# Attention and a two-layer projection: the products with V in one run per pair of heads, and a list scheduler with new durations and priorities

## The chip, the cores and the metric

One core of a Trainium2 chip runs the kernel. The metric is device time in microseconds, the median of the runs of one program; lower is better.

## The reference

Two parts follow each other. The first is attention for 8 batches and 8 heads, 576 tokens, head size 64, float32. A score counts where the query's block of 64 tokens is not ahead of the key's. The second takes the attention's result as 4608 tokens of 512 features. `w_in`, `w_out` and `g_ln` reach the chip as float64 words.

```python
scores = scale * np.matmul(q, k.transpose(0, 1, 3, 2))       # scale = 1/sqrt(64)
scores = np.where(block_i >= block_j, scores, -1000000000.0)
attn = np.exp(scores - np.max(scores, axis=-1, keepdims=True))
attn = attn / (np.sum(attn, axis=-1, keepdims=True) + 1e-09)
x = np.matmul(attn, v)                                       # then (tokens, 512)
h = x @ w_in                                                 # (4608, 1024)
e = np.exp(h - np.max(h, axis=-1, keepdims=True))
solu = h * (e / (np.sum(e, axis=-1, keepdims=True) + 1e-09))
mu, var = mean and variance of solu over its 1024 features
out = ((solu - mu) / np.sqrt(var + 1e-06) * g_ln) @ w_out    # (4608, 512)
```

## The kernel before

**Attention** (`attention(p)`, from L376) works on a pair of heads; there are 32 pairs, four to a batch. q and k are loaded and transposed on TensorE (L400). For the first four pairs the scores are float32 products (L441); for the others q and k are split into two float32r parts each, and the scores are sums of two products (L449, L445). VectorE takes each row's maximum (L469), ScalarE the exponential with its sum (L473), VectorE the reciprocal (L480, L481), and GpSimd scales the probabilities (L488; L489 is the same on VectorE, open for the first four pairs). 25 transposes in seven groups turn the probabilities around (L499); each group is copied from PSUM into `pt` by ScalarE (L371).

The **products with V** (L533) are float32, with 64 columns of weights: the two heads lie side by side in the array, which is used as two halves (128*64 in the profile; everything else is 128*128). The result of a pair has two parts, `ph` 0 (four products of two instructions) and `ph` 1 (ten products of two). Each part is an operation of its own, with its own PSUM slot and its own list of copies it waits for: `ph` 0 needs only the first two groups of transposes. The results go into `xt` (L371), which holds three batches.

**The projections** (`moe(t, key)`, from L549) take 36 tiles of 128 tokens. x is split into two float32r parts (`xh` L564 and `xl` L568), `h` is 24 matmuls in two halves (L589), then come maximum (L595), exponential (L596), product with its sum (L597), subtraction of the mean (L599), squares (L601), the reciprocal root (L612), eight transposes of `u` (L624, called `ct`), the split into `ch` and `cl` (L628, L629), 24 matmuls of `o` (L637), the scaling on the way out of PSUM (L641) and the store (L643).

**The weights** are prepared once, in 16 pieces (`prep`, L315 to L336): float64 words to float32 in five steps on ScalarE, VectorE and GpSimd (L322, L323, a scaling by 2^-112 at L324 to L326, L327, L328, L329), a product with g for `w_out` (L331, L332), a cast to the upper part (L333, L334) and a subtraction for the lower part (L335, L336). They use the tiles `ub`, `ob` and `xt[2]`, which the projections and the third batch need later.

**The order of all instructions** is set at build time by `Schedule`. Every operation has an engine, a duration, the tiles it reads and writes, and a key. `run` steps through modelled time; an engine that is free takes, among the operations whose inputs are ready and for which a PSUM slot is free, the one with the lowest key. `alts` names other engines that can do an operation, with a penalty added to the key; an alternative is only open if its penalty is under 3. PSUM has two slots of two banks ("D") and four of one bank ("S"). Each engine then runs its own list in that order, and waits by semaphores; SP issues nearly all loads. The key of an operation of attention is the pair's number p plus an offset of `PARAMS` (`K["pt"] + p` for the transposes of the probabilities, names with `32` for the first four pairs); that of an operation of tile t is `4 + K["h0"] + t * K["hs"]` plus an offset (`K["h"]`, `K["o"]`, `K["ct"]`); that of weight piece n is `K["w0"] + K["w1"] * n`. What the products with V add to the list in each pair:

```python
for ph in range(2):
    av = newps("S")
    js = range(5) if ph else range(2)
    ...
    sel = [c for c in ptc if (c[1] <= 6) == (ph == 0)]
    ptk = [(x, p % NPT, c0) for x in ("pt", "pt2") for c0, _ in sel]
    op("PE", 54 + sum(t_two(64 * mov(j, 0, ph)[2], True) for j in js), avmm, r=ptk + [f"vr{i}"], key=kk, opens=av)
```

Of the kernel before, what the change touches and what calls it, by code (L numbers as in the profile page):

```python
# [31 lines left out]
NPT = 2  # L32
START = {"PE": 0.0, "ACT": 2930.0, "DVE": 0.0, "POOL": 2500.0, "SP": 560.0}
PARAMS = {
# [6 lines left out]
    "a_sp32": -5.767, "a_lf": -3.555, "a_w": 15.208, "a_xh": 37.196, "a_xl": 48.757, "a_c": 6.341,  # L41
    "a_o": 13.796, "ns32": 4, "np": 32, "l0": -6.655, "a_cl": 5.076,
# [7 lines left out]
class Schedule:  # L50
    """Orders the operations of all engines: a list schedule over their dependences, with
    durations from shapes alone. PSUM slots (of one or two banks) are given out as it goes,
    and an operation that several engines can do goes to the one that is free for it first."""
# [10 lines left out]
    def op(self, eng, dur, fn, r=(), w=(), key=0.0, opens=None, ps=None, tail=0.0, alts=()):  # L64
# [3 lines left out]
        for e, d, f, pen in alts:  # L68
            if pen < 3:
                o.alts[e] = (d, f, key + pen)  # L70
        o.succ, o.npred, o.pre, o.opens, o.done = [], 0, [], opens, False
        o.idx = len(self.ops)
        o.uses = ps if ps is not None else opens
        preds = set()
        r, w = list(r), list(w)
        if o.uses is not None:
            self.users[o.uses] = self.users.get(o.uses, 0) + 1
            (w if eng == "PE" else r).append(("ps", o.uses))
# [18 lines left out]
    def run(self):  # L97
# [5 lines left out]
        engfree = {e: START[e] for e in engs}  # L103
        events = [(t, i, 0, None, None) for i, t in enumerate(sorted(START.values()))]
# [12 lines left out]
        while events:  # L117
            t = events[0][0]
            while events and events[0][0] <= t:
                _, _, kind, o, e = heapq.heappop(events)  # L120
                if kind == 1:
                    for s in o.succ:
                        s.npred -= 1
                        s.pre.append((t, o.eng))
                        if s.npred == 0:
                            ready(s, t)
                    if o.uses is not None:
                        left[o.uses] -= 1
                        if left[o.uses] == 0:
                            heapq.heappush(events, (t + LAT[o.eng]["PE"], n, 3, o, None))  # L130
                            n += 1
                elif kind == 2:
                    pend[e].append((o.alts[e][2], o.idx, o))
                elif kind == 3:
                    free[self.kind[o.uses]].append(self.slot[o.uses])
            for e in engs:
# [4 lines left out]
                for _, _, o in pend[e]:  # L141
                    if o.opens is not None:
                        if not free[self.kind[o.opens]]:
                            continue
                    elif o.uses is not None:
                        until = max([v for x, v in held[o.uses].items() if x != e], default=0.0)
# [11 lines left out]
                if best.opens is not None:  # L158
                    self.slot[best.opens] = free[self.kind[best.opens]].pop(0)
                    held[best.opens] = {}  # L160
                if best.uses is not None:
                    held[best.uses][e] = t + best.dur + 128
# [12 lines left out]
def kernel(  # L175
# [45 lines left out]
    # upper parts (its last 128 columns: 64 of the last queries, 64 zeros), then lower parts  # L221
# [4 lines left out]
    # tiles of queries: (head, i) is 128 rows of one head, LAST the last 64 of both heads  # L226
# [20 lines left out]
    # the scores of the first pairs are float32 products  # L247
# [14 lines left out]
    # the table of functions is loaded, and the clock of the tensor engine raised, while the  # L262
    # first loads are under way
# [16 lines left out]
    def newps(kind):  # L280
        vid[0] += 1
        sc.kind[vid[0]] = kind
        return vid[0]
# [4 lines left out]
    def t_mm(n):  # L288
        return max(107.0, n / 2.4 + 2.5)
# [4 lines left out]
    def t_two(n, fp32=False):  # L294
        # two products with 64 rows of output each, side by side in the array
        return max(224.0, n / 0.6 + 29) if fp32 else max(106.0, n / 2.4 + 53.0)
# [19 lines left out]
    def prep(i, src, hi, lo, gcol, name, key):  # L316
# [6 lines left out]
        op("DVE", 335, lambda: DVE.tensor_scalar(out=T2, in0=high, scalar1=TOP, scalar2=-TOP, op0=ALU.min, op1=ALU.max), r=[kr_], w=[k2], key=key)  # L323
        op("ACT", 520, lambda: ACT.activation(T2, T2, AF.Copy, scale=DOWN), r=[k2], w=[k2], key=key,  # L324
           alts=[("POOL", 588, lambda: POOL.tensor_scalar(out=T2, in0=T2, scalar1=DOWN, scalar2=1.0, op0=ALU.mult, op1=ALU.mult), K["a_cl"]),
                 ("DVE", 335, lambda: DVE.tensor_scalar(out=T2, in0=T2, scalar1=DOWN, scalar2=None, op0=ALU.mult), K["a_lf"])])  # L326
        op("DVE", 335, lambda: DVE.tensor_scalar(out=T1.bitcast(U32), in0=T2.bitcast(U32), scalar1=3, scalar2=0x7FFFFFF8, op0=ALU.logical_shift_left, op1=ALU.bitwise_and), r=[k2], w=[k1], key=key)  # L327
        op("DVE", 602, lambda: DVE.scalar_tensor_tensor(out=T1.bitcast(U32), in0=T2.bitcast(U32), scalar=0x80000000, in1=T1.bitcast(U32), op0=ALU.bitwise_and, op1=ALU.bitwise_or), r=[k1, k2], w=[k1], key=key)  # L328
        op("POOL", 1225, lambda: POOL.tensor_tensor(out=T1.bitcast(I32), in0=T1.bitcast(I32), in1=T3.bitcast(I32), op=ALU.add), r=[k1, k3], w=[k1], key=key)  # L329
        if gcol is not None:  # L330
            op("ACT", 613, lambda: ACT.activation(T1, T1, AF.Copy, scale=gcol), r=[k1, "gt"], w=[k1], key=key,  # L331
               alts=[("DVE", 400, lambda: DVE.tensor_scalar(out=T1, in0=T1, scalar1=gcol, scalar2=None, op0=ALU.mult), K["a_lf"])])  # L332
        op("ACT", 520, lambda: ACT.activation(hi, T1, AF.Copy), r=[k1], w=[(name, "h")], key=key,  # L333
           alts=[("DVE", 335, lambda: DVE.tensor_copy(hi, T1), K["a_lf"])])  # L334
        op("POOL", 1225, lambda: POOL.tensor_tensor(out=lo, in0=T1, in1=hi.bitcast(F32), op=ALU.subtract), r=[k1, (name, "h")], w=[(name, "l")], key=key,  # L335
           alts=[("DVE", 602, lambda: DVE.tensor_tensor(out=lo, in0=T1, in1=hi.bitcast(F32), op=ALU.subtract), K["a_w"])])  # L336
# [16 lines left out]
    # score tiles in PSUM: kind, [(unit, column)], [(first masked column, step, count)]  # L353
# [8 lines left out]
    # columns of the sums, by the two batches of reciprocals  # L362
# [6 lines left out]
    def copy(which, n_, aps, scale, w, key, ps, r=()):  # L369
        # a copy out of PSUM, on either engine  # L370
# [3 lines left out]
    def attention(p):  # L374
# [27 lines left out]
        # the last tile of kr is [k's last 64 tokens; q's last 64 tokens]  # L402
# [285 lines left out]
```

## Time and profile before

| | |
|---|---|
| median of 3 runs | 816.08 us (815.44 to 816.29) |
| span of the profiled execution | 814.3 us (its own time is not given beside it) |
| TensorE busy | 787.6 us, 97% |
| ScalarE busy | 557.0 us, 68% |
| VectorE busy | 492.3 us, 60% |
| GpSimd busy | 308.6 us, 38% |
| largest shares of the chain that ended last | `o` L637 24%, `h` L589 23%, products with V L533 10%, transposes of probabilities L499 9%, scores L449 8% |

The span runs from the first to the last instruction of one execution. A busy share is a mean over stages: the start, where weights are prepared and the first pairs run, the long middle, where a pair and a tile alternate, and the end, where only tiles are left. TensorE's matmuls are pipelined, so their durations overlap; what a matmul costs is read from the distance of starts, or from the chain of waits.

### The profile page before, as it was taken

What the parts mean: (1) busy time and instruction counts of PE and PEld (TensorE: products, weight loads), DVE (VectorE), ACT (ScalarE), POOL (GpSimd) and SP (SyncE); (2) the same over time, 40 slices, a digit from 0 to 9 for tenths busy, and PEclk for the clock granted to TensorE, in tenths of its full rate; (3) what the DMA queues carried; (4) which work ended last, traced back from release to release, by engine and by line L of the source; (5) the groups of instructions that cost most, each with busy time, mean ns of one, the idle gap of its engine ahead of it and who ended that gap; (6) DMA issues with size and microseconds to landing.
All of it is one profiled execution on the core that took longest, in us unless ns stands there. A gap on an engine that the chain in (4) does not pass through costs nothing.

```text
span 814.3 us, 14121 instructions
## 1 busy us (share of the span) xinstructions
PE 787.6 (97%) x4711; PEld 635.9 (78%) x4711; DVE 492.3 (60%) x1200; ACT 557.0 (68%) x1441; POOL 308.6 (38%) x468
## 2 busy tenths in 40 slices
PE   6878899999999999999999999999999999999998
PEld 5545678888888888888888888888888888788886
DVE  5999986655665555566665555555666655333332
ACT  6778787686877777777787777777777777434332
POOL 3567772243443323333333323233333333132210
PEclk9999999999999999999999999999999999999999
DMA  7457534143443343333333333433343320000000
GB/s 210 117 146 181 140 83 105 49 102 82 109 101 92 88 101 101 93 95 96 94 90 79 83 94 87 101 101 96 92 101 88 95 63 29 14 27 26 14 27 39
DMA packets 132760, 71.84 MB, mean 88 GB/s; under 512 B 118864, under 2 KB 118864, under 8 KB 132688
## 3 DMA queue, kind: packets, MB, share of 16 engines
q1 hardware_dynamic: 131632, 70.68, 34.0%
q8 instruction: 37, 0.61, 0.3%
q10 hardware_dynamic: 1056, 0.26, 0.2%
q14 instruction: 35, 0.29, 0.1%
HBM read 36.70 MB, written 9.44 MB: 57 GB/s over the span
## 4 chain that ended last, share of the span: by engine, by line
PE 86%; DVE 9%; issue 2%; ACT 1%; POOL 1%; DMA 0%; SPq 0%; DVEq 0%; POOLq 0%
PE ps L637 24%; PE ps L589 23%; PE ps L533 10%; PE ps L499 9%; PE ps L449 8%; PE ps L624 5%; PE ps L400 3%; PE ps L445 3%; DVE nm L469 2%; DVE pb L489 1%; DVE xt L326 1%; DVE xt L328 1%; DVE xt L327 1%; PE ps L441 1%; DVE ks L420 1%
## 5 line engine op out<-in xcount | busy, mean ns | idle before, releaser
L488 POOL TENSOR_SCALAR pb<-pb,rz 128x512 f32<-128x512 f32 (+4 forms) x270 | 148.8, 571 | 179.0 <-DVE rz L481 164.1
L473 ACT ACTIVATE pb<-ps,nm 128x128 f32<-128x128 f32 (+4 forms) x288 | 155.7, 551 | 61.6 <-DVE nm L469 61.5
L469 DVE TENSOR_REDUCE nm<-ps 128x1 f32<-128x128 f32 (+4 forms) x288 | 133.0, 504 | 4.3 <-PE ps L445 1.2
L599 POOL TENSOR_SCALAR ub<-ub,ms 128x1024 f32<-128x1024 f32 x36 | 41.0, 1140 | 190.0 <-DVE ms L598 190.0
L499 PE MATMUL ps<-ident,pb 128*128 128x128 f32 x800 | 106.0, 275 | 7.1 <-ACT pb L473 3.3
L371 ACT ACTIVATE pt<-ps 128x512 f32<-128x512 f32 (+1 forms) x224 | 108.7, 553 | 4.9 <-PE ps L499 4.3
L499 PEld LDWEIGHTS ps<-ident,pb 128*128 128x128 f32 x800 | 92.6, 141 | 23.3 <-ACT pb L473 3.6
L533 PE MATMUL ps<-pt,vr 128*64 128x320 f32 (+4 forms) x896 | 101.3, 366 | 0.7 <-ACT pt L371 0.5
L533 PEld LDWEIGHTS ps<-pt,vr 128*64 128x64 f32 x896 | 58.8, 137 | 41.7 <-issue 5.5
L449 PE MATMUL ps<-ks,qs 128*128 128x384 f32 (+1 forms) x448 | 84.5, 328 | 1.7 <-DMA qs<-qs 1.2
L589 PE MATMUL ps<-wih,xh 128*128 128x512 f32 x288 | 82.2, 407 | 2.9 <-DVE qtl L428 2.9
L637 PE MATMUL ps<-woh,ch 128*128 128x512 f32 x288 | 83.6, 411 | 0.0
L629 DVE TENSOR_TENSOR cl<-ps,ch 128x512 fp32r<-128x512 f32 x72 | 49.3, 685 | 56.6 <-ACT ch L628 56.6
L589 PE MATMUL ps<-wil,xh 128*128 128x512 f32 x288 | 79.6, 399 | 0.0
L637 PE MATMUL ps<-wol,ch 128*128 128x512 f32 x288 | 79.0, 396 | 0.0
L637 PE MATMUL ps<-woh,cl 128*128 128x512 f32 x288 | 78.8, 395 | 0.0
L589 PE MATMUL ps<-wih,xl 128*128 128x512 f32 x288 | 78.2, 393 | 0.0
L449 PEld LDWEIGHTS ps<-ks,qs 128*128 128x128 f32 x448 | 68.6, 191 | 7.2 <-ACT xh L564 1.0
L641 ACT ACTIVATE ob<-ps,ms 128x512 f32<-128x512 f32 x36 | 24.7, 687 | 71.5 <-PE ps L637 66.6
L596 ACT ACTIVATE ub<-ps,ms 128x1024 f32<-128x1024 f32 x36 | 40.1, 1115 | 46.2 <-DVE ms L595 46.1
L589 PEld LDWEIGHTS ps<-wil,xh 128*128 128x128 f32 x288 | 54.9, 191 | 12.9
L637 PEld LDWEIGHTS ps<-woh,cl 128*128 128x128 f32 x288 | 54.1, 188 | 13.0
(79 smaller groups left out, 1238.6 us busy)
## 6 DMA issues: line engine op xcount, KB each, us to landing
qs<-qs SPq DMA_DIRECT2D x56, 288.0 KB, 4.1
out_dram<-ob SPq DMA_DIRECT2D x36, 256.0 KB, 2.0
qr<-in_q_dram SPq DMA_DIRECT2D x64, 128.0 KB, 3.0
vr<-in_v_dram SPq DMA_DIRECT2D x64, 128.0 KB, 2.5
ks<-k2h SPq DMA_DIRECT2D x56, 144.0 KB, 2.5
kr<-in_k_dram SPq DMA_DIRECT2D x62, 128.0 KB, 2.7
ub<-in_moe_w_in_dram SPq DMA_DIRECT2D x8, 512.0 KB, 3.6
ub<-in_moe_w_out_dram SPq DMA_DIRECT2D x8, 512.0 KB, 3.7
```

The lines of the kernel that those rows point to most:

```text
L371: op("ACT", t_act(n_), lambda: ACT.activation(aps()[0], aps()[1], AF.Copy, scale=scale), r=r, w=w, key=key, ps=ps, alts=[("DVE", t_dve(n_) ...
L449: PE.matmul(t[:, off : off + wid[u]], qs[h][:, 640 * n_ + 128 * i_ : 640 * n_ + 128 * i_ + 128], ks[h][:, 0 : wid[u]], start=n_ == 0, stop ...
L469: op("DVE", t_dve(wid[u]), lambda sp=sp, off=off, u=u: DVE.tensor_reduce(out=nm_[u], in_=PS(sp)[:, off : off + wid[u]], axis=AX.X, op=ALU. ...
L473: op("ACT", t_act(wid[u], 186), lambda sp=sp, off=off, u=u, zg=zg, zc=zc: ACT.activation(pb[:, poff[u] : poff[u] + wid[u]], PS(sp)[:, off ...
L488: op("POOL", 0.836 * nn + 243, lambda b=b, nn=nn, zg=zg, zc=zc: POOL.tensor_scalar(out=pb[:, poff[b] : poff[b] + nn], in0=pb[:, poff[b] : ...
L499: PE.transpose(t[:, (s_ - c0) * P : (s_ - c0 + 1) * P], pb[:, poff[b] + j * P : poff[b] + (j + 1) * P], ident)
L533: PE.matmul(PS(av)[half[h], 64 * o_ : 64 * (o_ + n_)], vt[:, j, 64 * h : 64 * h + 64], pt_.rearrange("p s q -> p (s q)")[:, 128 * s_ + 64 ...
L589: PE.matmul(o_, a_[:, c, :], w_[:, c, s_], start=(si == 0 and c == 0), stop=(si == 2 and c == NKI - 1))
L599: op("POOL", 1097, lambda: POOL.tensor_scalar(out=u, in0=u, scalar1=m[:, 3:4], scalar2=1.0, op0=ALU.add, op1=ALU.mult), r=[uk, ("m3", i)], ...
L624: PE.transpose(t_[:, c * P : (c + 1) * P], u[:, (4 * hf + c) * P : (4 * hf + c + 1) * P], ident)
L629: op("DVE", t_dve(512), lambda cs=cs, cps=cps: DVE.tensor_tensor(out=cl[:, cs, :].rearrange("p c q -> p (c q)"), in0=PS(cps), in1=ch[:, cs ...
L637: PE.matmul(o_, a_[:, c, :], w_[:, c, :], start=(hf == 0 and si == 0 and c == 0), stop=(hf == 1 and si == 2 and c == 7))
```

## The change

1. The products with V of both parts become one operation: it opens two one-bank PSUM slots, waits for all seven copies of transposed probabilities, and issues its 28 instructions in a row.
2. `Schedule` can open several PSUM slots for one operation. It keeps the tiling that TensorE was last used in and adds `SWITCH` = 130 ns to an operation in the other one (`mode`). It treats GpSimd and the operations of VectorE marked `port` as users of one resource: while one runs, the other's aren't started.
3. Durations of the model: 24 matmuls of a projection at 231.5 ns instead of 216, scores and products with V by new formulas.
4. All offsets of `PARAMS` are new. Penalties that cross the bound of 3: `a_lf` (casts, the scaling by 2^-112 and the product with g on VectorE) -3.6 to 122.9, closed; `a_cl` (that scaling on GpSimd) 5.1 to -88.3, open; `a_w` (the weights' subtraction on VectorE) 15.2 to -51.8, open; `a_o` (the outputs' scaling on VectorE) 13.8 to -121.7, open.

Nothing that is computed changes, nor any shape of an instruction. The core of the diff:

```diff
+SWITCH = 130.0
 PARAMS = {
-    "nd": 2, "ld": 50.439, "lv": 1.808, "q": -3.52, "qe": 1.142, "s": 6.097, "se": -34.711, "sr": -9.155,
-    "sp": -24.637, "pt": -53.902, "pe": -29.441, "av": -40.478, "ae": -54.031, "x": -19.096, "h0": 30.197,
-    "hs": 1.049, "h": 10.087, "he": 5.197, "c": 29.273, "sq": 24.027, "ct": -50.339, "ce": -26.902,
-    "o": 12.508, "oe": 52.668, "w0": 4.753, "w1": 3.56, "q32": -49.338, "qe32": 2.512, "s32": -30.884,
-    "se32": -21.58, "sr32": -9.773, "sp32": 10.661, "pt32": -1.589, "pe32": 9.069, "av32": -26.682,
-    "ae32": -42.402, "ld32": 8.508, "lv32": 16.251, "e0": 19.063, "e1": 23.219, "e2": 43.479, "a_sp": 40.963,
-    "a_sp32": -5.767, "a_lf": -3.555, "a_w": 15.208, "a_xh": 37.196, "a_xl": 48.757, "a_c": 6.341,
-    "a_o": 13.796, "ns32": 4, "np": 32, "l0": -6.655, "a_cl": 5.076,
+    "nd": 2, "ld": 67.63, "lv": -39.691, "q": 8.023, "qe": 9.533, "s": -24.887, "se": -34.498,
+    "sr": -111.106, "sp": -24.343, "pt": -134.132, "pe": -125.475, "av": -34.899, "ae": -72.798,
+    "x": -37.528, "h0": -8.482, "hs": 0.492, "h": 132.7, "he": -68.376, "c": 83.463, "sq": 117.471,
+    "ct": -171.804, "ce": 39.0, "o": 33.813, "oe": 81.677, "w0": -14.772, "w1": 7.585, "q32": 2.115,
+    "qe32": -27.97, "s32": -13.067, "se32": -42.156, "sr32": 115.054, "sp32": 29.952, "pt32": 73.492,
+    "pe32": -3.409, "av32": -11.716, "ae32": -160.724, "ld32": 53.733, "lv32": 90.552, "e0": 39.854,
+    "e1": 108.665, "e2": 81.5, "a_sp": 145.727, "a_sp32": -6.778, "a_lf": 122.869, "a_w": -51.778,
+    "a_xh": 13.907, "a_xl": 186.098, "a_c": 45.054, "a_o": -121.701, "ns32": 4, "np": 32, "l0": -100.944,
+    "a_cl": -88.339,
 }
...
+                    port = e == "POOL" or e == "DVE" and o.port
+                    if port and portfree > t:
+                        heapq.heappush(events, (portfree, n, 0, None, None))
+                        n += 1
+                        continue
+                    if o.opens:
+                        kinds = [self.kind[x] for x in o.opens]
+                        if any(len(free[k]) < kinds.count(k) for k in kinds):
                             continue
...
+                if e == "PE" and best.mode != mode:
+                    best.dur += SWITCH
+                    mode = best.mode
+                if e == "POOL" or e == "DVE" and best.port:
+                    portfree = t + best.dur
...
-        for ph in range(2):
-            av = newps("S")
-            js = range(5) if ph else range(2)
-
-            def avmm(av=av, js=js, ph=ph):
+        avs = [newps("S"), newps("S")]
+
+        def avmm():
+            for ph, js in ((0, range(2)), (1, range(5))):
                 for j in js:
...
-            sel = [c for c in ptc if (c[1] <= 6) == (ph == 0)]
-            ptk = [(x, p % NPT, c0) for x in ("pt", "pt2") for c0, _ in sel]
-            op("PE", 54 + sum(t_two(64 * mov(j, 0, ph)[2], True) for j in js), avmm, r=ptk + [f"vr{i}"], key=kk, opens=av)
+        ptk = [(x, p % NPT, c0) for x in ("pt", "pt2") for c0, _ in ptc]
+        op("PE", sum(t_two(64 * mov(j, 0, ph)[2], True) for ph, js in ((0, range(2)), (1, range(5))) for j in js), avmm, r=ptk + [f"vr{i}"], key=kk, opens=tuple(avs), mode=1)
+        for ph in range(2):
+            av = avs[ph]
...
-            op("PE", 12 * 216, hmm, r=wk + [("xh", i), ("xl", i)], key=key + K["h"], opens=hps if hf == 0 else None, ps=hps)
+            op("PE", 12 * 231.5, hmm, r=wk + [("xh", i), ("xl", i)], key=key + K["h"], opens=hps if hf == 0 else None, ps=hps)
```

## Rows read from the trace of the kernel before

**Rows 1.** The page's first part: busy time, share of the span and instructions of each engine.

```profile
PE 787.6 (97%) x4711; PEld 635.9 (78%) x4711; DVE 492.3 (60%) x1200; ACT 557.0 (68%) x1441; POOL 308.6 (38%) x468
```

**Rows 2.** Busy time of each engine by stretches (start to end), granted clock, DMA share, GB/s.

```profile
0.00:20.00 20.00, 12.71 (x59) 9.83 (x60) 11.47 (x32) 12.29 (x33) 7.42 (x23) 1.00 0.79 210
20.00:40.00 20.00, 16.79 (x77) 11.51 (x77) 19.44 (x42) 14.55 (x39) 10.54 (x10) 0.92 0.47 123
40.00:60.00 20.00, 14.82 (x87) 9.39 (x88) 19.35 (x48) 15.89 (x51) 13.23 (x12) 1.00 0.48 129
60.00:80.00 20.00, 16.75 (x128) 11.79 (x128) 19.56 (x36) 17.08 (x43) 14.21 (x15) 0.95 0.72 184
80.00:100.00 20.00, 16.89 (x85) 12.50 (x82) 19.53 (x37) 13.62 (x38) 16.19 (x17) 0.88 0.54 138
100.00:120.00 20.00, 19.50 (x125) 15.60 (x124) 18.01 (x44) 18.01 (x47) 15.15 (x18) 1.00 0.34 84
...
426.00:448.40 22.40, 22.40 (x143) 18.42 (x142) 13.48 (x35) 16.35 (x44) 7.95 (x13) 1.00 0.38 94
```

**Rows 3.** Chain of waits, 400 to 475 us: start us, us, what (a pair's products, L533).

```profile
430.27 0.80 PE ps L533 x8
431.07 0.59 PE ps L624 x4
431.66 2.21 PE ps L533 x20
```

**Rows 4.** Chain of waits, 780 to 815 us: same columns.

```profile
786.34 5.59 PE ps L589 x24
...
801.20 0.44 PE ps L624 x4
```

**Rows 5.** TensorE: line L533 alone (ns min/median/max, first and last), then timeline 0 to 150 us.

```profile
L533 PE MATMUL ps<-pt,vr x896: 218/381/797, 30.4 to 701.1; 128*64 128x320 f32 x76, 128*64 128x256 f32 x26, 128*64 128x128 f32 x26, 128*64 128x192 f32 x26
...
61.70 2.93 PE L533 MATMUL ps<-pt,vr 128*64 128x320 f32 x28 [0.49 <-ACT pt L371]
64.56 2.62 PE L499 MATMUL ps<-ident,pb 128*128 128x128 f32 x19
```

**Rows 6.** The page's groups: copies of transposed probabilities out of PSUM (busy, mean ns).

```profile
L371 ACT ACTIVATE pt<-ps 128x512 f32<-128x512 f32 (+1 forms) x224 | 108.7, 553 | 4.9 <-PE ps L499 4.3
```

**Rows 7.** Instructions by line, 0 to 115 us: count, busy us, mean ns, idle before.

```profile
L326 DVE TENSOR_SCALAR xt<-xt 128x512 f32<-128x512 f32 x16 | 14.4, 918 | 0.1
...
L328 DVE SCALAR_TENSOR_TENSOR xt<-xt 128x512 uint32<-128x512 uint32 x16 | 12.1, 758 | 0.1
...
L322 ACT ACTIVATE ob<-ub 128x512 int32<-128x512 uint32 x16 | 10.7, 679 | 0.0
...
L334 DVE CAST woh<-xt 128x512 fp32r<-128x512 f32 x5 | 4.6, 917 | 0.1
...
L332 DVE TENSOR_SCALAR xt<-xt,gt 128x512 f32<-128x512 f32 x4 | 4.2, 1054 | 0.0
...
L334 DVE CAST wih<-xt 128x512 fp32r<-128x512 f32 x4 | 1.7, 413 | 0.4 <-POOL xt L329 0.4
```

**Rows 8.** The page's DMA issues: count, KB each, median us to landing.

```profile
qr<-in_q_dram SPq DMA_DIRECT2D x64, 128.0 KB, 3.0
```

**Rows 9.** Timeline, all engines, 426 to 449 us and 795 to 815 us: start us, us.

```profile
426.70 1.23 DVE L597 SCALAR_TENSOR_TENSOR ub<-ps,ub 128x1024 f32<-128x1024 f32 x1
...
430.52 1.12 POOL L599 TENSOR_SCALAR ub<-ub,ms 128x1024 f32<-128x1024 f32 x1 [5.75 <-DVE ms L598]
...
445.89 1.23 DVE L595 TENSOR_REDUCE ms<-ps 128x1 f32<-128x1024 f32 x1
...
447.15 1.11 ACT L596 ACTIVATE ub<-ps,ms 128x1024 f32<-128x1024 f32 x1 [1.14 <-DVE ms L595]
...
802.30 0.69 DVE L629 TENSOR_TENSOR cl<-ps,ch 128x512 fp32r<-128x512 f32 x1 [0.70 <-ACT ch L628]
```

**Rows 10.** Busy time by stretches again, one short stretch (columns as in rows 2).

```profile
64.50:68.60 4.10, 4.02 (x33) 3.07 (x29) 4.04 (x8) 4.04 (x12) 3.83 (x4) 1.00 0.73 162
```

More of the change, by code (lines that the diff above doesn't have):

```diff
@@ L62, in __init__, with op @@
         self.kind = {}
-    def op(self, eng, dur, fn, r=(), w=(), key=0.0, opens=None, ps=None, tail=0.0, alts=()):
+    def op(self, eng, dur, fn, r=(), w=(), key=0.0, opens=None, ps=None, tail=0.0, alts=(), port=False, mode=0):
         o = Op()
@@ L70, in op @@
                 o.alts[e] = (d, f, key + pen)
+        o.port, o.mode = port, mode
         o.succ, o.npred, o.pre, o.opens, o.done = [], 0, [], opens, False
         o.idx = len(self.ops)
-        o.uses = ps if ps is not None else opens
+        o.opens = () if opens is None else opens if isinstance(opens, tuple) else (opens,)
+        o.uses = o.opens if ps is None else (ps,)
         preds = set()
         r, w = list(r), list(w)
-        if o.uses is not None:
-            self.users[o.uses] = self.users.get(o.uses, 0) + 1
-            (w if eng == "PE" else r).append(("ps", o.uses))
+        for x in o.uses:
+            self.users[x] = self.users.get(x, 0) + 1
+            (w if eng == "PE" else r).append(("ps", x))
         for b in r:
@@ L103, in run @@
         engfree = {e: START[e] for e in engs}
+        portfree, mode = 0.0, 0
         events = [(t, i, 0, None, None) for i, t in enumerate(sorted(START.values()))]
@@ L126, in run @@
                             ready(s, t)
[L127 to L130, printed above, removed]
+                    for x in o.uses:
+                        left[x] -= 1
+                        if left[x] == 0:
+                            heapq.heappush(events, (t + LAT[o.eng]["PE"], n, 3, x, None))
                             n += 1
@@ L134, in run @@
                 elif kind == 3:
-                    free[self.kind[o.uses]].append(self.slot[o.uses])
+                    free[self.kind[o]].append(self.slot[o])
             for e in engs:
@@ L141, in run @@
                 for _, _, o in pend[e]:
-                    if o.opens is not None:
-                        if not free[self.kind[o.opens]]:
+                    port = e == "POOL" or e == "DVE" and o.port
[6 more added lines that the diff above has]
+                        if any(len(free[k]) < kinds.count(k) for k in kinds):
                             continue
-                    elif o.uses is not None:
-                        until = max([v for x, v in held[o.uses].items() if x != e], default=0.0)
+                    elif o.uses:
+                        until = max([v for x, v in held[o.uses[0]].items() if x != e], default=0.0)
                         if until > t:
@@ L157, in run @@
                 best.dur, best.fn, _ = best.alts[e]
[L158 to L162, printed above, removed]
+                if e == "PE" and best.mode != mode:
[3 more added lines that the diff above has]
+                    portfree = t + best.dur
+                for x in best.opens:
+                    self.slot[x] = free[self.kind[x]].pop(0)
+                    held[x] = {}
+                for x in best.uses:
+                    held[x][e] = t + best.dur + 128
                 best.t = t
@@ L294, in t_two @@
     def t_two(n, fp32=False):
-        return max(224.0, n / 0.6 + 29) if fp32 else max(106.0, n / 2.4 + 53.0)
+        return max(214.0, n / 0.6) if fp32 else max(106.0, n / 2.4 + 53.0)
     def t_act(n, extra=0.0):
@@ L639, in moe @@
             wk = [(f"wo{c}", x) for c in range(4 * hf, 4 * hf + 4) for x in "hl"]
-            op("PE", 12 * 216, omm, r=wk + [("ch", hf), ("cl", hf), ("ch2", hf)], key=key + K["o"], opens=ops_ if hf == 0 else None, ps=ops_)
+            op("PE", 12 * 231.5, omm, r=wk + [("ch", hf), ("cl", hf), ("ch2", hf)], key=key + K["o"], opens=ops_ if hf == 0 else None, ps=ops_)
         op("ACT", t_act(512, 93), lambda: ACT.activation(ob[i], PS(ops_)[:, 0:DM], AF.Copy, scale=m[:, 3:4]), r=[("m3", i)], w=[("ob", i)], key=key + K["oe"], ps=ops_,
```

26 lines of the change are left out of this document (13 added, 13 removed).

## The prediction, made before the changed kernel was run

> **What bounds the kernel now.** I read the page first: TensorE is busy 97% of the span, the next engine 68% [rows 1]. A share over the whole span hides stages, so the second view is the table of stretches [rows 2]. The reader should see two regimes. From 120 us on TensorE is busy for the whole stretch (22.40 of 22.40 us at 426 us), while VectorE is busy 13.48 us and ScalarE 16.35 us of it: only the time that TensorE needs for its own instructions counts there. In the first 120 us TensorE idles 7.3 + 3.2 + 5.2 + 3.3 + 3.1 + 0.5 = 22.5 us, and from 20 to 100 us it is VectorE that is full (19.4, 19.4, 19.6, 19.5 of 20). So there are two places to gain: a shorter instruction stream after 120 us, and less VectorE work before it.
>
> The third view is the chain of waits in the steady part [rows 3]. A pair's products with V come there in two runs, 8 instructions in 0.80 us and 20 in 2.21 us, with four transposes between them that take 0.59 us. Four transposes of the same form take 0.44 us in the tail, where no product with V is near [rows 4].
>
> **Part 1, one run of products per pair.** Products with V use half-width weights (128*64), everything else 128*128. Twice in the first 75 us the old order happens to set 28 such products back to back (the second run of one pair, then the first of the next); the first time they take 64.56 - 61.70 = 2.86 us [rows 5]. Split, the same 28 take 0.80 + 2.21 = 3.01 us [rows 3], 0.15 more; and the transposes between them lose 0.59 - 0.44 = 0.15. So a run costs about 0.30 us for going into the other tiling and coming back, whoever its neighbours are. 896 products [rows 5] are 32 pairs of 28; the timeline of TensorE has them in 62 runs from 30.4 to 701 us (30 of 8, 30 of 20, two of 28), and the change makes 32. Removed: 30 x 0.30 = **9.0 us**, all of it on TensorE, nearly all of it where TensorE is the bound. Bounds: 4.5 us if the transposes' half goes elsewhere, 9.0 if it doesn't; I take 9.0, since nothing in the 22.40 us stretch would absorb it.
>
> The run now needs all seven copies of transposed probabilities and two of the four one-bank PSUM slots at once; before, its first eight products needed two copies and one slot. On TensorE, which works in order, scores, transposes and projections queue behind it; the copies into xt, then the split of x, wait for its end. I cost this at nothing in the steady part: what hides it are the 24 input-projection matmuls of a tile (5.59 us, [rows 4]), which by the new keys are TensorE's last choice and so its filler. If that cover is gone, a wait is one copy, 0.55 us [rows 6], and a bank's release behind it; I keep that as a rival.
>
> **Part 2, the new keys and alternatives in the first 120 us.** An alternative is open only if its penalty is under 3. `a_lf` goes from -3.6 to 122.9: VectorE loses the scaling by 2^-112 (L326, 14.4 us), nine casts (L334, 4.6 + 1.7) and four products with g (L332, 4.2), together 24.9 us [rows 7]. `a_w` goes to -51.8: VectorE may take up to 16 subtractions of L335; no row shows that form on VectorE, the nearest is L328, two SBUF inputs of the same size, 0.76 us [rows 7]: 0 to 12.1 us. Its 107.4 us of 120 [rows 2] become 82.5 to 94.6. ScalarE must take the casts and the products with g, 13 x 0.68 (L322, the same size, [rows 7]) = 8.8 us, and of the 16 scalings those that GpSimd doesn't: 0 to 10.9. Its 91.4 us become 100 to 111. So the fuller of the two engines goes from 107.4 us to somewhere from 100 to 111: a gain of 7 to a loss of 4. `a_cl` (-88) puts the scaling at the head of GpSimd's choices, and GpSimd is busy for only 76.7 of these 120 us, so I take a quarter of them on ScalarE, 103 us: **-4 us**. SP's order changes too: the weight loads now come ahead of the first pairs' q, k and v loads. Their pieces still wait for two buffers, so a pair's load finds SP free in between; I cost it at nothing, and at one load's landing, 3.0 us [rows 8], if not.
>
> The cast of L334 takes 413 ns in one group and 917 ns in the other, with the same shape, and L326 averages 918: VectorE is held up in some of these [rows 7]. The Trainium skill, page "SBUF — State Buffer", section "Who interferes with whom", has it that VectorE and GpSimd share a pair of SBUF ports, which one of them holds for its whole instruction. By that rule a scaling moved to GpSimd still keeps VectorE waiting, the start would gain nothing, and the sum would be 809 us, inside the forecast's own range; the row alone, which counts VectorE's time, gives the 805 below.
>
> **Part 3, the outputs' scaling.** `a_o` (-121.7) moves up to 36 instructions of L641 from ScalarE to VectorE. Both have slack beside a full TensorE [rows 2]; cost nothing, and some 0.7 us at the very end if the last one changes engine for the worse.
>
> **Part 4, the tail.** With attention done, TensorE picks among the transposes (`ct`), the output projection (`o`) and the input projection (`h`). Before, h of tile t+2 (key 44.3 + 1.05(t+2)) beat o of tile t (46.7 + 1.05t), so the last h ended at 786.34 + 5.59 = 791.9 us with three tiles of o left to fill TensorE [rows 4]. The new keys put every o (29 + 0.5t) ahead of every h (128 + 0.5t). When the last h ends at most one tile of o is left, and the last tile's own chain lies open: maximum 1.23, exponential 1.11, product 1.23, subtraction 1.12 [rows 9], 4.7 us, and five handovers that I put at 0.15 each, 5.5 us; then from the transposes at 801.20 [rows 4] to the end of that half's cl at 802.30 + 0.69 = 802.99 [rows 9], 1.8; some 7.3 us in all. One o (5.6 us) left beside it leaves 1.7, none leaves 7.3. Bounds 0 to 7.3; I take **+2**, the row of one tile left, because two tiles are in flight in turn.
>
> **Sum**, against the profiled execution: its span is 814.3 us; the page gives no time of its own beyond that, and the median of the runs, 816.1, lies 1.8 above, which I take to lie around the span. 814.3 - 9.0 - 4 + 2 = 803.3; with 1.8, **805 us**. About 0.2% (1.6 us) is what a measurement of this kernel can tell from no change.
>
> **Rivals.**
> *The start opens up.* The 22.5 us of idle time holds 7.3 in the first 20 us, where loads and the first pair run alone; the other 15.2 could all go if ScalarE, VectorE and GpSimd are evenly loaded. For it: VectorE is full and ScalarE is not [rows 2]. Against: with its new work ScalarE is at 100 to 111 us of the 120 (part 2). 816.1 - 9.0 - 15.2 + 2 = 794.
> *Two banks and seven copies starve TensorE* (the slower end). Place: ahead of every run of 28. Price: the last copy of probabilities and one copy that still holds the second bank, 0.55 us each [rows 6]: 1.10 - 0.30 = 0.80 a pair, 32 x 0.80 = 26; with parts 2 and 4, 840 us. It decides from 0.30 us of waiting per pair. Against: TensorE does not idle at all at 426 us, and the filler is 5.6 us per tile.
> *Both ends against it.* Start +4, tail +7.3, run -9.0: 818, or about no change if one of them is a little milder.
> *The runs are joined and nothing is gained,* because the cost is at the seam between the two results and not in the tiling: 814. Against: the back-to-back case shows no seam [rows 5].
> *TensorE's clock.* It was granted less than full in stretches of the start in which TensorE stood idle part of the time (0.92, 0.95, 0.88, [rows 2]), that is, its lower level (1.2 GHz) for a part of them; from 64.5 to 68.6 us it did nothing but transposes, right behind a run of 28, and was granted 1.00 [rows 10]. The Trainium skill, page "TensorE: Matmul & The Clock Gate", section "Part 4: PE-mode transpose", says that transposes do not count as activity for the clock. By that rule a run of 28 next to 25 transposes could lose the clock. As a mechanism here: a loss like that of 80 to 100 us, 0.12 x 20 = 2.4 us, in each of 32 pairs would be +77, 882 us; the row at 64.5 us speaks against it.
>
> **How the numbers follow.** Forecast 0.66, the start opening up 0.13, starved TensorE 0.08, both ends against it 0.06, nothing gained 0.04, clock 0.03. Low end 795: the start's rival, nearly whole. High end 814: start +4, tail +2 and a run's gain of 7.5 come to 814.6, nothing gained to 814. What is left out is the starved case, the clock and both ends against it, 0.17. Faster: 0.66 + 0.13 + 0.04 = 0.83; half of both ends within 0.2%, 0.03; slower 0.14.
>
> **What would show it.** Right: 32 runs of 28 products in about 2.86 us; a stretch like the 22.40 us of one pair and one tile 0.3 us shorter, TensorE full in it; VectorE under 18 us of 20 between 20 and 100 us, L326 on ScalarE or GpSimd; 1 to 3 us without TensorE work after the last h. Wrong: idle time of TensorE ahead of L533 after 120 us, idle time over 22 us before it, or more than three idle microseconds at the end.

## The result, and the profile after

The changed kernel takes 820.32 us (median of 4 runs, 818.74 to 820.8), the kernel before 816.15 us beside it: a ratio of 1.0048, with a 95% interval of 1.0033 to 1.0062. It is slower, by 4.2 us, where 805 was forecast. The line numbers of the changed kernel are 16 or 17 higher: products with V L549 (were L533), `ct` L641 (L624), the subtraction of the mean L616 (L599), `h` L606, `o` L654. An edit of an experiment can shift them by one or two more.

The page's first part (busy time, share of the span, instructions), which answers to [rows 1]: TensorE is busy for 3.8 us less, in a span 2.6 us longer.

```profile
PE 783.8 (96%) x4711; PEld 635.4 (78%) x4711; DVE 478.9 (59%) x1194; ACT 551.8 (68%) x1446; POOL 301.9 (37%) x469
```

Busy time by stretches of the changed kernel, columns as in [rows 2], with the stretch from 426 us, as there, in the last row:

```profile
0.00:120.00 120.00, 102.19 (x617) 75.79 (x618) 93.98 (x231) 104.58 (x284) 67.00 (x93) 0.97 0.59 152
120.00:150.00 30.00, 28.60 (x168) 24.25 (x167) 23.52 (x56) 23.41 (x56) 16.28 (x26) 1.00 0.48 117
150.00:700.00 550.00, 540.76 (x3409) 443.92 (x3408) 312.15 (x807) 385.09 (x1036) 191.95 (x314) 1.00 0.35 86
700.00:820.00 120.00, 112.25 (x523) 91.41 (x521) 49.20 (x102) 38.66 (x72) 26.69 (x37) 0.99 0.06 22
...
426.00:448.40 22.40, 22.02 (x140) 18.10 (x140) 12.93 (x33) 15.72 (x43) 7.95 (x13) 1.00 0.37 92
```

The reader should see where the idle time of TensorE went. In the first 120 us it fell from 22.5 us [rows 2] to 17.8, as forecast; 1.4 us of it came back from 120 to 150 us, where the kernel before had none. But from 150 to 700 us, where the kernel before had 0.4 us of it (549.64 of 550), there are now 9.2 us. The waits of that stretch say ahead of what (engine, line, whom it waited for: us in all, times, longest; PE is TensorE's matmul, PEld its weight load):

```profile
PEld ps L641 <- POOL ub L616: 14.7, 23, 0.8
...
PE ps L641 <- POOL ub L616: 9.2, 23, 0.6
```

Once in each pair TensorE waits for GpSimd's subtraction of the mean before it can transpose the tile. The wait is seen in two rows. From the start of the four transposes ahead of `ct` to the start of those behind it the mean is 1.93 us here, and 1.31 us in the run `qtl_later` below, where `ct` waits for nothing: one of these waits costs 0.62 us, and 23 of them 14.3 us. So the row of the weight load (14.7 us) holds about the whole of this loss, and the matmul's row (9.2 us) a part of it. The chain of waits (start, us, what) shows what is behind it; for [rows 3] the engine there was TensorE throughout.

```profile
428.08 2.86 PE ps L549 x28
430.93 0.68 PE ps L466 x4
...
432.75 1.46 ACT pb L490 x5
...
435.11 0.55 ACT k2h L433
435.69 0.69 DVE ks L437
...
436.45 0.76 DVE ks L437
...
437.24 1.23 DVE ms L612
438.47 0.03 issue
438.50 0.68 DVE qs L445
439.18 0.13 DVE qtl L445
...
439.35 0.69 DVE qs L445
440.04 0.14 DVE qtl L445
...
440.21 1.23 DVE ub L614 x2
441.44 0.08 DVE ms L621
...
442.03 0.07 DVE ms L615
442.10 0.08 issue
442.18 1.13 POOL ub L616
443.31 0.05 issue
443.36 1.09 PE ps L641 x8
...
450.80 2.86 PE ps L549 x28
```

This is a closed loop of one pair. The 28 products stand in one run of 2.86 us, as forecast. The scores behind them release the maxima and exponentials; behind these, in the order of their own engines, come the copy and the splits of the next k and q, the tile's maximum (L612), its product (L614), three small instructions for the reciprocal (L621 to L623), the mean (L615) and the subtraction (L616); and `ct` starts 0.05 us after that. The next run starts 450.80 - 428.08 = 22.72 us after this one; before it was 22.37 us.

Before, this loop was open by a whole pair: a subtraction L599 ran from 430.52 to 431.64 us [rows 9], while the transposes at 431.07 [rows 3], already under way, belonged to the tile ahead of it. Its own came with the next run, at 453.44 us: 21.8 us of room. The first two rows are from the chain of waits before, the third from TensorE's timeline after:

```profile
419.18 2.78 PE ps L589 x12
...
453.44 0.59 PE ps L624 x4
...
433.27 1.17 PE L606 MATMUL ps<-wih,xh 128*128 128x512 f32 x4
```

With the new keys (`ct` from -50.3 to -171.8, `h` from 10.1 to 132.7) nearly all of that room is gone, and from both sides. Counted from the start of the pair's products, `ct` came 23.2 us after it and now comes 15.3 us after it. The subtraction came 0.25 us after it and now comes 14.1 us after it, since the second half of the tile's `h`, which began 11.1 us ahead of the products (419.18), now begins 5.3 us behind them (433.27). So 13.9 us of the room went because the subtraction is later, and 7.9 because `ct` is earlier.

The plan that the changed kernel's code makes expects this order to run without a wait. In it a pair takes 22.05 us, the subtraction ends 14.55 us after the start of the products, and `ct` follows 0.29 us later, of which 0.135 is the model's handover from GpSimd to TensorE. On the chip the subtraction ended 443.31 - 428.08 = 15.23 us after that start, 0.68 us later than planned. In the plan of the kernel before, `ct` had 20.5 us of room.

### The profile page after: what moved, and what is told of

Same layout as the page of the kernel before. It is cut to its first block, busy times and chain, and to the rows that moved or that the text cites. A ratio compares the mean times of both kernels' runs of the same rounds, so it can differ in the third digit from the quotient of the medians.

```text
span 816.9 us, 14273 instructions
## 1 busy us (share of the span) xinstructions
PE 783.8 (96%) x4711; PEld 635.4 (78%) x4711; DVE 478.9 (59%) x1194; ACT 551.8 (68%) x1446; POOL 301.9 (37%) x469
## 4 chain that ended last, share of the span: by engine, by line
PE 50%; DVE 22%; ACT 13%; issue 5%; DMA 4%; POOL 4%; SPq 1%; DVEq 0%; ACTq 0%; POOLq 0%
PE ps L606 15%; PE ps L549 9%; ACT pb L490 7%; PE ps L654 6%; PE ps L466 6%; PE ps L516 5%; DVE qs L445 4%; PE ps L641 4%; DVE ks L437 4%; DVE ub L614 4%; DVE ms L612 4%; POOL ub L616 3%; PE ps L462 2%; DVE nm L486 2%; PE ps L458 2%
## 5 line engine op out<-in xcount | busy, mean ns | idle before, releaser
L505 POOL TENSOR_SCALAR pb<-pb,rz 128x512 f32<-128x512 f32 (+4 forms) x267 | 146.0, 566 | 222.9 <-DVE rz L498 213.6
L490 ACT ACTIVATE pb<-ps,nm 128x384 f32<-128x384 f32 (+4 forms) x288 | 155.9, 574 | 25.3 <-DVE nm L486 25.2
L486 DVE TENSOR_REDUCE nm<-ps 128x1 f32<-128x384 f32 (+4 forms) x288 | 137.1, 513 | 8.5 <-PE ps L462 2.5
L388 ACT ACTIVATE pt<-ps 128x512 f32<-128x512 f32 (+1 forms) x224 | 111.8, 564 | 2.6 <-PE ps L516 2.4
L516 PE MATMUL ps<-ident,pb 128*128 128x128 f32 x800 | 108.8, 274 | 4.4 <-ACT xt L388 1.2
L482 DVE MEMSET ps<- 64x128 f32 (+1 forms) x160 | 22.0, 144 | 130.0 <-PE ps L466 124.9
L549 PE MATMUL ps<-pt,vr 128*64 128x320 f32 (+4 forms) x896 | 93.2, 360 | 0.0
L549 PEld LDWEIGHTS ps<-pt,vr 128*64 128x64 f32 x896 | 59.1, 137 | 39.8 <-ACT pb L490 8.4
L388 ACT ACTIVATE xt<-ps 64x128 f32<-64x128 f32 (+3 forms) x160 | 42.8, 312 | 64.6 <-PE ps L549 64.1
L606 PE MATMUL ps<-wih,xh 128*128 128x512 f32 x288 | 82.8, 408 | 1.1 <-ACT pb L490 1.1
L654 PE MATMUL ps<-woh,ch 128*128 128x512 f32 x288 | 80.9, 402 | 0.6 <-ACT ch L645 0.6
L606 PE MATMUL ps<-wil,xh 128*128 128x512 f32 x288 | 79.0, 396 | 0.0
L654 PE MATMUL ps<-wol,ch 128*128 128x512 f32 x288 | 78.7, 395 | 0.0
L654 PE MATMUL ps<-woh,cl 128*128 128x512 f32 x288 | 78.5, 394 | 0.0
L606 PE MATMUL ps<-wih,xl 128*128 128x512 f32 x288 | 78.3, 393 | 0.0
L616 POOL TENSOR_SCALAR ub<-ub,ms 128x1024 f32<-128x1024 f32 x36 | 40.5, 1125 | 78.0 <-DVE ms L615 75.0
L490 ACT ACTIVATION_READ_ACCUMULATOR pb<-ps,nm 128x1 f32 x288 | 65.8, 228 | 0.0
L585 POOL TENSOR_TENSOR xl<-xt,xh 128x512 fp32r<-128x512 f32 (+1 forms) x40 | 47.4, 1190 | 46.6 <-PE ps L606 29.2
```

The costliest lines, as they stand in the source:

```text
L388: op("ACT", t_act(n_), lambda: ACT.activation(aps()[0], aps()[1], AF.Copy, scale=scale), r=r, w=w, key=key, ps=ps, alts=[("DVE", t_dve(n_) ...
L486: op("DVE", t_dve(wid[u]), lambda sp=sp, off=off, u=u: DVE.tensor_reduce(out=nm_[u], in_=PS(sp)[:, off : off + wid[u]], axis=AX.X, op=ALU. ...
L490: op("ACT", t_act(wid[u], 186), lambda sp=sp, off=off, u=u, zg=zg, zc=zc: ACT.activation(pb[:, poff[u] : poff[u] + wid[u]], PS(sp)[:, off ...
L505: op("POOL", 0.836 * nn + 243, lambda b=b, nn=nn, zg=zg, zc=zc: POOL.tensor_scalar(out=pb[:, poff[b] : poff[b] + nn], in0=pb[:, poff[b] : ...
L516: PE.transpose(t[:, (s_ - c0) * P : (s_ - c0 + 1) * P], pb[:, poff[b] + j * P : poff[b] + (j + 1) * P], ident)
L549: PE.matmul(PS(avs[ph])[half[h], 64 * o_ : 64 * (o_ + n_)], vt[:, j, 64 * h : 64 * h + 64], pt_.rearrange("p s q -> p (s q)")[:, 128 * s_ ...
```

## The experiments

All ratios are to the kernel before, run on the same chip beside the experiment.

**The join alone.** The kernel before keeps its keys and its list, but the second run of each pair is moved up to the first, as far as its inputs allow (35 runs in all).

```diff
+        order = sc.run()
+        for first, second in zip(avs[::2], avs[1::2]):
...
+            order.insert(i + 2 + last, order.pop(j))
```

> The kernel before, its finished list kept, with the second run of a pair's products with V moved up to directly behind the first wherever no other operation's data or PSUM slot forbids it: 35 runs instead of 62, all else in the old order. Theory A (a run costs 0.30 us for its two changes of tiling; the loss of the changed kernel comes from its order, in which the transposes ct wait 0.62 us per pair for GpSimd's ub): 27 x 0.30 = 8.1 us less, 808 us, and no new wait of TensorE after 120 us. Rival B (joining is itself the loss: the run needs all copies and two slots, so TensorE waits ahead of it or behind it): 815 us or more, with idle time ahead of the products with V or of ct in each pair.

Measured: 842.64 us, ratio 1.0327 (1.0311 to 1.0342): not theory A's 808. Rival B's 815 or more came, at a place that it hadn't named. The run itself was as short as hoped (2.86 us), but the scores behind the `ct` that follows it now wait, twice per pair, for PSUM banks: one that the tile's `ch` and `cl` must release, one that the copies into `xt` must release. The waits of TensorE from 150 to 700 us:

```profile
PE ps L450 <- DVE cl L630: 11.5, 22, 0.9
PE ps L450 <- ACT xt L372: 7.6, 19, 0.4
```

Scores read neither `cl` nor `xt`, so what they wait for is the banks. The prediction's second rival (840) named a price close to this, with the old keys in place of the new ones; its place was wrong: behind the run, not ahead of it.

**The same with the copies first.** ScalarE's copies into `xt` go ahead of its squares (L602).

```diff
+        for o_ in [o_ for o_ in order if o_.eng == "ACT" and o_.fn.__code__.co_firstlineno == 602]:
...
+                    order.insert(i, order.pop(j))
```

> joined_old_order with ScalarE's copies of a pair's second result part moved ahead of the squares (L602, 1.1 us) that stood in front of them, so that their PSUM bank is free earlier. In joined_old_order the second group of scores waited for VectorE's cl and the third for these copies, some 0.7 us each per pair. Theory E (joining there fails for lack of one-bank slots: two of the run and two of ct are taken when the scores want three): the third group's wait goes, 24 x 0.65 = 15 us less, 827 us, and the second's stays. Rival: the wait is for something else (the order on TensorE), 840 us or more.

Measured: 846.64 us, 1.0375 (1.0362 to 1.0388), where theory E had 827 and its rival 840 or more. The wait for `xt` went, that for `cl` stayed (13.2 us), and a new one came: transposes of k and q wait for exponentials (L401 for L474, 7.3 us in 19 waits), which the copies had pushed back. A change of one place in this list was not enough.

**The new operations with the old keys.** The changed kernel, `PARAMS` as before.

```diff
-    "nd": 2, "ld": 67.63, "lv": -39.691, "q": 8.023, "qe": 9.533, "s": -24.887, "se": -34.498,
...
+    "nd": 2, "ld": 50.439, "lv": 1.808, "q": -3.52, "qe": 1.142, "s": 6.097, "se": -34.711, "sr": -9.155,
```

> The changed kernel with the old PARAMS: joined runs, new durations, the charge per change of tiling and the shared port stay. Theory A: the join is worth 9 us whatever the keys; if this list has no wait in its steady part, 807 us, and if its ct or another operation stands at the end of a chain planned too short, some 0.6 us x 23 more, 821 us: the profile's waits of TensorE decide. Rival B: 815 us or more with waits ahead of the products with V. Rival C (the new keys alone are the loss, by the start): 807 us, with the gain over the changed kernel in the first 120 us.

Measured: 834.68 us (831.83 to 840.73), 1.0212 (1.0195 to 1.0229): rival B's 815 or more, but with the waits at another place than it had them. The profile is of the longest run. The scheduler, though it knows that a run needs two banks, makes a list with waits ahead of scores, too (L465 for the q transfer 5.1 us, for `pt` 3.0, for `ch` 2.5), and the start is worse as well (22.9 us without TensorE work in the first 120, against 17.8). The new keys are what makes the join bearable: some 14 us.

**Longer VectorE durations in the model.** From 435.69 to 441.44 us the chain above has eight VectorE instructions, 5.75 us. The code's `t_dve` (n/0.96 + 65 ns) gives them 2 x 0.665 + 1.132 + 2 x (0.598 + 0.132) + 1.132 = 5.05, that is 0.70 less. If such an error were all, a plan with 0.1 us more per instruction would place `ct` right.

```diff
-        return n / 0.96 / rate + 65.0
+        return n / 0.96 / rate + 165.0
```

> The changed kernel with one constant of its model raised: t_dve(n) = n/0.96 + 165 instead of + 65 ns, near what the profile shows for the VectorE operations of the chain (1.23 us for 1024 columns, 0.69 for 512); the planner makes a new list from it. Theory A (ct is placed at the planned end of a chain that is planned some 0.6 us too short): no wait of ct in the steady part, 14 us less, 806 us, give or take 4 us since start and end are planned anew. Rival B (the joined run itself): the steady distance between pairs stays at 22.7 us and the time at 815 or more.

Measured: 826.39 us, 1.0129 (1.0114 to 1.0144): worse, and rival B's signs came, 815 or more and still 22.75 us from one run of products to the next (430.12 to 452.87). But the whole order is another: the new plan gives `ct` 15.5 us of room, the wait at `ct` is gone, and scores wait instead, for transfers of q (8.2 us in 15 waits) and for `pt` (3.4). That tells nothing for or against the loop, because everything moved; so the next edits leave the list as it is and move single instructions.

**The mean ahead of the reciprocal.** On VectorE, L615 goes ahead of the three instructions L621 to L623, which only the later scaling needs. They stand between the product (from 440.21) and the mean (from 441.94 on VectorE's timeline). In one early tile the mean lands ahead of the product it is taken from, so this tile's output is another.

```diff
+        for o_ in [o_ for o_ in order if o_.fn.__name__ == "rz"]:
+            m3 = sc.ops[o_.idx - 3]
+            if order.index(m3) > order.index(o_):
+                order.remove(m3)
+                order.insert(order.index(o_), m3)
```

> The changed kernel, its finished list kept, with VectorE's small operation L615 (the mean's factor, which GpSimd's L616 waits for) put ahead of the three small ones L621 to L623 that stand in front of it; TensorE, ScalarE, GpSimd and SP have the same lists. Theory A (ct waits for ub at the end of a chain over ScalarE, VectorE and GpSimd): L615 comes about 0.5 us earlier, the wait of ct falls from 0.62 to 0.1 to 0.2 us per pair, 23 pairs x 0.5 = 11 us less, 809 us. Rival B (the joined run starves TensorE) and rival C (the loss sits in the start's keys): 819 to 821 us, since neither touches this.

Measured: 810.48 us, 0.9931 (0.9912 to 0.9951). The same without that one tile:

```diff
+            if order.index(m3) > order.index(o_) > order.index(sc.ops[o_.idx - 4]):
```

> As m3_first, but L615 is moved only where the product L614 that it reads already stands ahead of it: in m3_first one tile near the start had it ahead of L614, so that tile's outputs were not the reference's. Theory A: the same time as m3_first within 2 us, 809 to 812.

Measured: 811.03 us, 0.9942 (0.9927 to 0.9956): 9.3 us less than the changed kernel, from the order of four tiny VectorE instructions, in an engine that is busy 59% of the time. The mean now starts 1.34 us after the product's start (434.87 to 436.21), where it took 1.73: the loop is 0.39 us shorter, and the wait of 0.62 us per pair fell to 0.25. The chain of waits is TensorE throughout, with a trace of the wait left (1.09 us for the eight transposes, where they alone take 0.87, see below):

```profile
422.72 2.85 PE ps L549 x28
...
437.17 0.44 PE ps L516 x4
437.61 0.04 issue
437.64 1.09 PE ps L641 x8
...
445.12 2.85 PE ps L549 x28
```

A pair now takes 445.12 - 422.72 = 22.40 us.

**Fill the wait instead.** The changed kernel, with four transposes of probabilities put ahead of `ct`, and then both moves together.

```diff
+            if [x.fn.__name__ for x in pe[n_ : n_ + 4]] == ["ctrans", "ctrans", "ptrans", "ptrans"]:
...
+                        order.insert(i, order.pop(j))
```

> The changed kernel's finished list, with one or both of the groups of transposes of the probabilities that follow ct moved ahead of ct on TensorE, where data and PSUM slots allow it (one of the two, 0.44 us, in the steady part); VectorE, ScalarE, GpSimd and SP keep their order. Theory A: TensorE has 0.44 us of work during the 0.62 us for which ct waits, so 23 x 0.44 = 10 us less, 810 us. Rival D (the wait of ct is one of several that end together, and the next takes its place): under 4 us less, 816 or more.

> m3_first_but_one and pt_before_ct together. Theory A: the 0.23 us per pair that m3_first left ahead of ct are covered by the 0.44 us of transposes: no wait of ct, 23 x 0.62 = 14 us below the changed kernel, 806 us, and a distance of 22.1 us between pairs. Rival D: not below m3_first, 810 us.

Measured: 821.32 us, 1.0055 (1.0039 to 1.007), and 820.96 us, 1.0059 (1.0042 to 1.0076). The filler has a wait of its own: its bank is still held by the result of `o`, until ScalarE has scaled it. In the run with both moves, from 150 to 700 us:

```profile
PEld ps L517 <- ACT ob L659: 14.5, 23, 0.6
PE ps L517 <- ACT ob L659: 9.0, 23, 0.4
```

That is what rival D said: two waits lay behind one another, some 0.6 us each, and the first hid the second. With `ct` ahead, the bank comes free while it transposes; so the order of the plan is the better one of the two, and its loop too long.

**The loop 0.4 us shorter still.** On top of `m3_first_but_one`, the two subtractions of 64 columns (`qtl`, L445, 0.13 and 0.14 us and their gaps) go behind L615.

```diff
+        for o_ in [o_ for o_ in order if getattr(o_, "half", None) is not None]:
...
+            i, j = order.index(o_), order.index(m3[0])
...
+                order.insert(j, order.pop(i))
```

> Edit: the kernel of m3_first_but_one, and in each pair of the steady part the two subtractions of 64 columns for q (L445, second of the two) are moved on VectorE from ahead of the product with its sum (L614) to behind the subtraction of the mean (L615). Theory (the chain from scores to ct over VectorE, ScalarE and GpSimd sets the end of the wait ahead of ct, and TensorE has nothing to fill it with): the chain gets about 0.4 us shorter, what was left of the wait, 0.25 us x 23, goes: 811.0 - 5.8 = 805, a pair about 22.15 us. Rival (the wait is only the first of several that lie close behind one another, as pt_before_ct showed for its bank): the moved subtractions or the bank behind them become the wait, 810 or more, with an idle time of TensorE at another place.

Measured: 806.68 us (804.93 to 809.6), 0.989 (0.9872 to 0.9909): the shortest time here, 1.1% below the kernel before. Its six runs lie in two groups, three at 805.0 and three from 808.3 to 809.6, with granted clocks of 0.996 and 0.992; the profile is of the first group. Its chain of waits in the steady part has no engine but TensorE; `ct` follows the transposes ahead of it at once and takes 0.87 us:

```profile
421.18 2.85 PE ps L550 x28
...
435.63 0.44 PE ps L517 x4
436.07 0.87 PE ps L642 x8
...
443.33 2.85 PE ps L550 x28
```

A pair takes 443.33 - 421.18 = 22.15 us, and there is no row left for a wait of `ct` in the view of the waits.

**What the change of tiling costs.** Again on `m3_first_but_one`, one more 128x128 transpose per pair, into the bank that the 20 products overwrite: once between the 8 and the 20, once ahead of the 28.

```diff
             for ph, js in ((0, range(2)), (1, range(5))):
+                if ph == 1:
+                    PE.transpose(PS(avs[1])[:, 0:P], ident, ident)
                 for j in js:
```

```diff
         def avmm():
+            PE.transpose(PS(avs[1])[:, 0:P], ident, ident)
             for ph, js in ((0, range(2)), (1, range(5))):
```

> Edit: the kernel of m3_first_but_one with one more 128x128 transpose per pair, between the first 8 and the other 20 products with V, into the bank that the 20 overwrite. Theory (going into the half-width tiling and back costs 0.30 us per run): the transpose itself costs about 0.11 us, the split 0.30, and 32 x 0.41 = 13 us: 824. Rival (the 0.30 us had another cause than the tiling): 32 x 0.11 = 3.5 us: 814.5, the same as transpose_ahead.

> Edit: the same additional transpose per pair, but directly ahead of the run of 28 products, so that no run is split. Theory and rival alike: 32 x 0.11 = 3.5 us over 811.0: 814.5. What tells them apart is the difference to transpose_between: 32 x 0.30 = 9.6 us by the theory, under 3 us by the rival.

Measured: 821.42 us (820.26 to 821.96) and 813.91 us (812.85 to 815.21). The chain of waits of the first,

```profile
430.26 0.80 PE ps L551 x8
431.06 0.26 PE ps L547
431.32 2.20 PE ps L551 x20
```

and of the second:

```profile
426.32 0.11 PE ps L545
426.43 2.85 PE ps L550 x28
```

The same instructions take 0.80 + 0.26 + 2.20 = 3.26 us split and 0.11 + 2.85 = 2.96 us unsplit: 0.30 us for one change of tiling and back, the figure of the forecast. Over 32 pairs that is 9.6 us; the medians differ by 7.5. The expected 824 came out 2.6 us lower and 814.5 0.6 lower, so the theory holds and its rival (under 3 us) doesn't. Four transposes between other 128*128 instructions take 0.44 us [rows 4], 0.11 each, so it isn't the mere change from products to a transpose that costs.

## Why the prediction was wrong

**The step that failed** is in part 1: "I cost this at nothing in the steady part: what hides it are the 24 input-projection matmuls of a tile". The part on the new keys asked what they do in the first 120 us and in the tail, and never what they do between. There were two errors in it.

- *The cover.* `h` is TensorE's last choice in the scheduler's modelled time, when the list is made. On the chip the list is fixed: TensorE, held up at `ct`, had no way to take `h` first. The term put at nothing measured 0.62 us per pair, 14.3 us in all, and `h` as the last choice had its part in it: the tile's subtraction, which needs `h`, came 13.9 us later in the pair. A list that is full in the model has no filler for what the model has wrong.
- *The place.* I looked for the new wait at the run of 28. There no matmul waited after 150 us; only the load of its weights did, 8.4 us in 23 waits, and as much in `qtl_later` (8.5), where TensorE is full. The new wait came at `ct`: 21.8 us of room became 0.05, and the loop over three other engines, 0.68 us longer than planned where the plan had 0.16 to spare, set the pair's time.

The size follows: 22.72 us per pair in place of 22.37 - 0.30 = 22.07, 0.65 us in each of some 23 pairs, is 15 us, the way from 805 to 820. Of the 0.65, 0.57 go with the wait (22.15 us a pair in `qtl_later`; on the mean of the 23 pairs it was 0.62), and 0.08 are a run that saved less than its 0.30. The reverse is shown: shorten only that loop, by 0.4 us and then by another 0.4, and the time goes to 811.0 and to 806.7. The profiled execution of the last one has a span of 803.1 us; the forecast's sum was 803.3 before the 1.8 around the span. That they agree so closely is in part luck: the run saved less than forecast, the tail cost less than forecast, and three of that kernel's six runs are 3.3 us or more longer.

**The other steps:**

- *The run, -9.0.* One run of 28 takes 2.86 us, and a split costs 0.30 us (the two transposes). What the join gives where nothing waits is less, 22.37 - 22.15 = 0.22 us per pair. The run's neighbours are now `h` and scores and no longer transposes; whether that is the missing 0.08 was not tried.
- *The tiling as the cause.* The Trainium skill, page "TensorEngine Tiling (Array Packing)", section "Key Properties", says that changing the tiling mode drains TensorE. The 0.30 us for the inserted transpose agree with it; the page gives no price. What in the change of tiling takes the time, no run here shows.
- *The start, -4.* TensorE's idle time there fell by 4.7 us, or by 3.3 with the 1.4 from 120 to 150 us. From 60 to 100 us its granted clock is 1.00, where it was 0.95 and 0.88 [rows 2]; what that gives was not forecast and is not told apart. VectorE has 93.98 us (forecast 82.5 to 94.6) and ScalarE 104.58 (100 to 111). Of the scalings 13 went to GpSimd and 2 to ScalarE, by the lines of the first 115 us; a quarter had been put on ScalarE.
- *The shared ports.* The Trainium skill, page "SBUF — State Buffer", section "Who interferes with whom", has GpSimd and VectorE lock each other out, from which I had worked out a start that gains nothing. The start gained, so that result was wrong for this case. The rule itself isn't tested by it, since the new scheduler's plan keeps such instructions apart: L345, which was L328, went from 758 [rows 7] to 708 ns.
- *The outputs' scaling, 0.* Of the 36 scalings 10 went to VectorE, and no row of them stands among the waits of TensorE in the changed kernel.
- *The tail, +2.* In place of 1.7 open microseconds there are two short waits of TensorE, 0.22 us ahead of the last `ct` and 0.57 ahead of the last `o`, with one `o` beside the chain as assumed. TensorE's idle time after 700 us grew by 0.8 us (3.8 to 4.6).
- *The rivals.* Starved TensorE (840) is near what the join does in the old order, 842.6, though by waits behind the run; it isn't what happens with the new keys. "Nothing gained" is refuted by the inserted transposes. "Both ends against it" gave 818 for causes that didn't come. The clock was granted at 1.00, the upper level (2.4 GHz), from 24.42 us on to 700, also around 54 and 73 us, where runs of 28 stand next to 31 and 25 transposes. From 150 us on the run's neighbours are `h` and scores.

Of the signs named beforehand, "idle time of TensorE ahead of L533 after 120 us" was the right kind with the wrong line. I gave the slower end 0.14; with every offset new, and a list whose room nobody had measured, that was too little.

## What to carry to other kernels

In a kernel whose instruction order is fixed at build time, "another engine hides it" holds only for work that stands *ahead of* the wait in that order. So, for every step that a change of priorities moves, read from the trace how long its input had been ready before; that room is what the model's errors use up first. And where a full engine waits once per iteration for a closed loop over engines that are half idle, take everything out of the loop that it doesn't need: here five small instructions of VectorE were worth 14 us.

## What the runs showed of the hardware

A wait of TensorE ahead of a transpose shows nearly whole at the load of weights and only in part at the matmul: of the 0.62 us lost per pair the load has 0.64 (14.7 us in 23 waits) and the matmul 0.38 (at 443.36 us). At the remaining 0.25 us of `m3_first_but_one` the matmul's rows show no idle time at all; the load does (6.2 us in 23 waits), and so does the group that takes 1.09 us in place of 0.87. But a wait of the load need not be a loss: ahead of the products it has 8.5 us in 23 waits in `qtl_later`, where the matmuls show no idle time from 150 to 700 us. So what a wait costs is best taken from the distances of the matmuls' starts. A VectorE instruction on 1024 elements held the next one back for 1.26 us (437.24 to 438.50), where the code had 1.13.
